# Memory-augmented attention beside a SiLU layer: weight pieces issued earlier, x tiles loaded from another queue, a new order of the work

## The chip, the cores and the metric

The kernel runs on one core of one Trainium2 chip. The core has a matrix engine (PE, with its weight loads shown apart as PEld), a vector engine (DVE), an activation engine (ACT), a general engine (POOL) and a sync engine (SP); each works through its own instructions in order, and semaphores join them. DMA transfers are issued from the queue of one of the engines, here SP and, for two tiles, ACT. The metric is the device time of one execution in microseconds, as the median of several runs; less is better.

## The reference

The input x has 2048 rows of 512 values. It is normalised once, and the result goes to an attention with a running memory and to a dense layer with SiLU. Both outputs are added to x. All data is bf16.

```
xn = _layernorm(x, axis=-1)
return x + _A_ref(xn, A_wq, A_wk, A_wv, A_wo, A_beta) + _B_ref(xn, B_w1, B_w2)
...
for s in range(N):                                  # N = 4 segments of 512 rows, 32 heads of 16
    logits = einsum('bhqd,bhkd->bhqk', qs, ks) * scale + mask
    a_dot = einsum('bhqk,bhkd->bhqd', softmax(logits), vs)
    a_mem = einsum(phi(qs), M) / (einsum(phi(qs), z) + 1e-06)
    o = g * a_mem + (1.0 - g) * a_dot
    M = M + einsum(phi(ks), vs);  z = z + sum(phi(ks))
...
out = einsum('bsf,fd->bsd', silu(einsum('bsd,df->bsf', xn, w1)), w2)      # 512 -> 1792 -> 512
```

Here phi(t) is t + 1 for positive t and exp(t) otherwise, and g is the sigmoid of beta, per head.

## The kernel before

The rows are taken in 16 tiles of 128, four tiles to a segment. The order of all work is written out by hand in the string ORDER (line 16): each word names a piece, the numbers behind it say of which segment, tile or part, and the loop at line 895 calls the pieces in that order. Every engine gets its instructions in this order and works them off one by one; an engine can run ahead of the others as far as its semaphores let it. So a word that only issues a DMA from SP runs when SP comes to it, which may be long before PE comes to the word that follows.

The words, as far as the prediction needs them:

- `xs`, or `xc` and `xd`: mean and variance of a tile of x on DVE (lines 283 to 292). `xq` and `xi` make the reciprocal root of the first four tiles on ACT and DVE (301, 304), `xg` that of four tiles at once on POOL (294). `Nv` normalises a tile on DVE (312). `X` and `Xa` or `Xv` turn the first four tiles on PE and copy them (831, 838); `XD` turns each of the others by a DMA transpose on SP (847).
- `k`, `q`, `v`, `h`: the products with wk, wq, wv and w1 on PE, in two or four parts; `ka`/`kv`, `qa`/`qv`, `va`/`vv` copy them out on ACT or DVE; `ha` (tanh, line 482) and `hv` make SiLU on ACT and DVE. `K` masks k by head on POOL (377).
- `S`: one of 72 batches of scores (line 699). Its products go into `psS`, of which there is one (line 701, four of the eight banks of the accumulator memory); ACT then takes the exponential of all 128 x 2048 values (721), and POOL clears what the causal mask forbids (735). `E` and `O` multiply 16 times each by v (line 760), `Ev`/`Ea` and `Ov`/`Oa` copy the result.
- `fa`, `ga`: exponentials of k and q for phi on ACT; `t`, `m`, `mv`, `mw`: the memory; `s`, `r`, `R`, `w`, `W`, `z`, `d`, `n`: sums, reciprocals and weights, with DMAs on SP that spread them.
- `o`, `oc`, `od`: products with w2 (index 0 to 13) and wo (14 to 17) for an output tile, with all 512, with 256 and with 128 columns (line 618); `oh` is a half of the last tile. `xl` loads a tile of x again to be added (601), `st` adds and stores a tile (606), `sh` half of the last one (653).
- `lw0.k` and `lw1.k` issue the loads of piece k of w2 and of wo on SP (883). `busy` gives PE products on zeros until the first real work (852). `kind`, `odd`, `omask`, `bmask` make small constants on DVE, `tb` has the table of the exponential loaded (307).

The products of the other words use four narrow products of 32 columns of weights beside each other, or one whole one, as the loop at line 895 finds it; listed by shape, a product of 512 columns has a mean of 380 ns either way. Scores are tiled by rows, so each S changes the tiling and changes it back.

At the start, SP issues tiles 0 and 2 of x, ACT tiles 1 and 3, each ahead of the weights wv, wk, wq, w1 and the other tiles of x on SP (lines 163 to 184). The first activation on ACT comes later, in line 211, a root of a constant that POOL makes; it brings the table load with it.

Of the kernel before, what the change touches and what calls it, by code (L numbers as in the profile page):

```python
# [25 lines left out]
S12 v1.1.3 fa0.3 Ov0 q1.0.0 q1.0.1 vv1.1 hv0.6 E1 k1.2.0 k1.2.1 k1.2.2 Ev1
S7 lw0.1 h0.7.0 fv0.0 q1.1.0 q1.1.1 q1.0.2 k1.2.3 kv1.2 h0.7.1 q1.1.2 q1.1.3 q1.0.3 qv1.1 fa0.2
S9 h0.5.0 h0.5.1 h0.5.2 h0.5.3 h0.8.0 h0.8.1 Nv8 Nv11 XD11 qv1.0 fv0.3 lw0.13 Nv10 XD8 XD10 ha0.5 hv0.5 t0.3 h0.7.2 lw1.3 fp0.2 h0.8.2 h0.8.3 ha0.8 Om0 hv0.8
S10 gp1.1 q1.2.0 q1.2.1 q1.2.2 h0.7.3 Nv9 ha0.7 q1.2.3 k1.0.0 qv1.2 lw0.5 lw1.2 k1.0.1 k1.0.2 XD9 k1.0.3 h0.10.0 kv1.0
S13 h0.10.1 O1 hv0.7 Ov1 q1.3.0 q1.3.1 q1.3.2 k1.3.0 q1.3.3 qv1.3 ga1.1  # L30
S11 fv0.2 h0.10.2 fp1.0 k1.3.1 t0.2 t0.0 k1.3.2 k1.3.3 xs15 kv1.3 h1.1.0 h1.1.1 h0.10.3 k1.1.0 lw0.0 ha0.10 h1.1.2 h1.1.3 ha1.1 hv0.10
S15 k1.1.1 hv1.1 h0.9.0 h0.9.1 h0.9.2 E2 K1.0 h0.9.3 ha0.9 h1.2.0 xs14 gv1.1 hv0.9 h1.2.1
S14 h1.2.2 h1.2.3 Ev2 k1.1.2 k1.1.3 kv1.1 xs12 ha1.2 hv1.2 O2 k2.2.0 lw0.4
S17 h1.10.0 h1.10.1 k2.2.1 kv2.2 lw1.0 h1.10.2 h1.10.3 ha1.10 gate h0.11.0 h0.11.1 h0.11.2 Ov2
S16 h0.12.0 h0.11.3 ha0.11 h0.12.1 h0.12.2 hv1.10 E3 Om2 Ev3 lw0.2 lw0.7 xl0.0 K1.1 hv0.11 k2.1.0 h0.12.3 ha0.12 K1.2
S20 k2.1.1 h0.13.0 h0.13.1 h0.13.2 kv2.1 hv0.12 O3 fp1.2 Ov3 m0.2 mv0.2 h0.13.3 fa1.0 Om1
S18 q2.1.0 q2.1.1 v2.2.0 m0.0 qv2.1 v2.2.1 lw0.3 ha0.13 fv1.0 K1.3
S19 mv0.0 k2.0.0 k2.0.1 hv0.13 v2.1.0 v2.1.1 kv2.0 fa1.2 h1.11.0
S22 vv2.2 sv0 r0.1 q2.3.0 lw0.8 vv2.1 h1.11.1 h1.11.2 xs13 xg12.4 o0.2.12 h1.11.3 q2.3.1 ha1.11 hv1.11 o0.2.7
S24 qv2.3 o0.2.4 lw0.11 od0.2.11.2 h1.8.0 h1.8.1 h1.8.2 h1.8.3 o0.2.13 h1.0.0 lw0.6 oc0.2.6.0 o0.2.1 od0.2.11.1 ha1.8 r0.2 r0.0  # L40
S25 E4 o0.2.2 h1.0.1 r0.3 w0 o0.2.8 z0.1 h1.0.2 h1.0.3 xl0.2 ha1.0 z0.2 hv1.8 Ev4 od0.2.11.0 h1.7.0 Nv15
S21 hv1.0 K2.1 h1.4.0 h1.7.1 h1.4.1 fv1.2 h1.7.2 h1.7.3 ha1.7 Nv12 XD12 hv1.7 q2.0.0 q2.0.1 XD15
S23 o0.2.3 qv2.0 h1.4.2 h1.4.3 ha1.4 o0.2.0 od0.2.11.3 fp1.1 z0.0 zv0.1 O4 z0.3 Ov4 k2.3.0
S26 zv0.2 fp1.3 k2.3.1 h1.9.0 h1.9.1 h1.9.2 h1.9.3 hv1.4 ha1.9 o0.0.8 K2.0 kv2.3 hv1.9 o0.0.5 o0.0.15
S31 E5 o0.0.4 bmask o0.0.2 od0.0.1.1 oc0.0.3.0 oc0.0.7.1 h1.13.0 Ev5 o0.0.10 fa1.3 h1.13.1
S28 Om3 O5 o0.0.6 Ov5 o0.0.13 Nv13 od0.0.1.0 o0.0.9 h1.13.2 h1.13.3 ha1.13 hv1.13 h1.3.0
S27 oc0.0.7.0 fv1.3 h1.3.1 oc0.0.3.1 h1.3.2 h1.3.3 xl0.3 od0.0.1.2 oc0.2.6.1 zv0.0 h1.12.0 ha1.3 h1.12.1 h1.12.2 hv1.3 XD13 gp1.2 t1.3 h1.12.3 ha1.12 hv1.12 Om5 oc0.2.10.1
S29 zv0.3 od0.0.1.3 o0.0.12 oc0.2.10.0 o0.0.16 o0.0.0 o0.2.15 o0.2.16 E6 fa1.1 o0.3.9 o0.3.15
S30 o0.3.16 o0.2.5 Ev6 o0.3.17 o0.3.6 o0.2.9 fv1.1 o0.1.14 o0.2.14 gp2.3 o0.2.17 st0.2 od0.1.8.3 t1.1 ga1.2 od0.1.8.1 gv1.2 oc0.3.1.1 gp1.0
S33 oc0.1.9.1 o0.0.17 o0.3.0 o0.3.12 Nv14 od0.1.8.0 o0.0.11 o0.1.17 XD14 o0.1.15 o0.0.14 t1.2 st0.0 ga1.0 gv1.0 t1.0 o0.3.14 od0.3.2.1  # L50
S32 O6 Ov6 o0.1.7 v2.0.0 o0.1.11 v2.0.1 vv2.0 oc0.3.3.1 ga2.3 fp2.1 gv2.3
S35 q2.2.0 q2.2.1 o0.1.3 qv2.2 o0.1.16 E7 Ev7 fa2.1 oc0.1.9.0
S34 mw0.0 fv2.1 o0.3.7 h1.6.0 o0.3.10 h1.6.1 o0.3.8 od0.3.2.2 od0.3.2.0 Om4 h1.6.2 h1.6.3 oc0.1.2.1 o0.3.11 ha1.6 hv1.6 gp1.3
S40 mw0.2 ga1.3 K2.3 o0.1.1 o0.3.4 O7 Ov7 gv1.3 q3.1.0 q3.1.1 xl0.1 qv3.1 oc0.3.3.0
S42 k3.1.0 o0.1.10 o0.3.13 k3.1.1 kv3.1 oc0.3.1.0 od0.3.2.3 oc0.1.2.0 o0.3.5 m1.2 mv1.2
S36 o0.1.13 o0.1.4 ga2.2 st0.3 od0.1.8.2 s1 sv1 gp2.2 v2.3.0 o0.1.5 K2.2 xl1.1 o1.2.12 r1.0 o0.1.0 m1.0
S37 fp2.0 v2.3.1 o0.1.12 Om6 mv1.0 vv2.3 o0.1.6 o1.2.10 Om7 q3.3.0 fa2.0 q3.3.1
S38 r1.1 qv3.3 h2.8.0 h2.8.1 v3.3.0 t2.1 ha2.8 v3.3.1 r1.3 r1.2 w1 o1.2.8 z1.3
S39 st0.1 hv2.8 od1.2.0.0 od1.2.0.2 vv3.3 z1.1 q3.2.0 q3.2.1 E8 Ev8 v3.0.0 d1.3
S41 qv3.2 v3.0.1 h2.11.0 o1.2.1 d1.2 h2.11.1 k3.0.0 ha2.11 zv1.3  # L60
S49 vv3.0 h1.5.0 h1.5.1 fv2.0 t2.0 h1.5.2 h1.5.3 ha1.5 hv2.11 o1.2.3 gv2.2 k3.0.1 kv3.0 z1.2 E9 hv1.5
S44 fp2.2 k3.2.0 ga2.1 k3.2.1 o1.2.13 xl1.2 v3.2.0 v3.2.1 Ev9 kv3.2 dv1.3
S43 vv3.2 zv1.1 h2.7.0 n1.3 nv1.3 gp2.1 h2.7.1 ha2.7 zv1.2 q3.0.0 q3.0.1
S48 qv3.0 d1.1 d1.0 O8 Ov8 o1.2.6 dv1.2 h2.5.0 h2.5.1 ha2.5 hv2.7 o1.2.4 oc1.2.11.1
S45 oc1.2.2.1 z1.0 K3.2 O9 hv2.5 h2.1.0 Ov9 dv1.0 h2.1.1 dv1.1 ha2.1 h2.12.0
# [868 lines left out]
```

## Time and profile before

| | us |
|---|---|
| median of 3 runs (221.83 to 222.88) | 221.88 |
| the profiled execution | 220.66 |
| its span | 218.9 |
| busy in it: POOL | 126.9 |
| busy in it: DVE | 180.0 |

The median is that of unprofiled executions; rows of the profile belong to the profiled execution, whose span runs from its first to its last instruction. All times of rows count from the start of that span. Busy shares say which engine is loaded over the whole; where the time goes is read from the chain of waits and from the timeline, which lists instructions in order of start, with several of a kind merged ("x8"). In a row "out<-in" are the tiles written and read, and in brackets stands the idle time ahead of it and what ended it.

### The profile page before, as it was taken

What the parts mean: (1) busy time and instruction counts of PE and PEld (TensorE: products, weight loads), DVE (VectorE), ACT (ScalarE), POOL (GpSimd) and SP (SyncE); (2) the same over time, 40 slices, a digit from 0 to 9 for tenths busy, and PEclk for the clock granted to TensorE, in tenths of its full rate; (3) what the DMA queues carried; (4) which work ended last, traced back from release to release, by engine and by line L of the source; (5) the groups of instructions that cost most, each with busy time, mean ns of one, the idle gap of its engine ahead of it and who ended that gap; (6) DMA issues with size and microseconds to landing.
All of it is one profiled execution on the core that took longest, in us unless ns stands there. A gap on an engine that the chain in (4) does not pass through costs nothing.

```text
span 218.9 us, 9451 instructions
## 1 busy us (share of the span) xinstructions
PE 213.7 (98%) x4081; PEld 116.7 (53%) x4081; DVE 180.0 (82%) x367; ACT 184.0 (84%) x174; POOL 126.9 (58%) x189
## 2 busy tenths in 40 slices
...
DMA packets 33530, 19.62 MB, mean 90 GB/s; under 512 B 14928, under 2 KB 33488, under 8 KB 33488
## 3 DMA queue, kind: packets, MB, share of 16 engines
...
q10 hardware_dynamic: 288, 0.26, 0.4%
q14 instruction: 10, 0.08, 0.1%
...
## 4 chain that ended last, share of the span: by engine, by line
PE 88%; ACT 8%; issue 2%; DVE 0%
PE ps L335 21%; PE psO L337 17%; PE ps L337 16%; PE psS L715 10%; PE psO L335 9%; PE psV L782 8%; ACT Pb L721 4%; PE psS L337 4%; PE psS L855 2%; ACT th L482 1%; ACT ex L413 1%; PE psM L442 1%; ACT L308 1%; ACT xnT L842 0%; ACT Vz L396 0%
## 5 line engine op out<-in xcount | busy, mean ns | idle before, releaser
L721 ACT ACTIVATE Pb<-psS 128x2048 bf16<-128x2048 f32 x72 | 135.2, 1878 | 4.0 <-PE psS L715 2.7
L735 POOL TENSOR_SCALAR_AFFINE_SELECT Pb<-Pb 128x512 bf16<-128x512 bf16 (+1 forms) x72 | 60.5, 841 | 29.6 <-ACT Pb L721 26.8
L487 DVE SCALAR_TENSOR_TENSOR hT<-th,ps 128x512 bf16<-128x512 bf16 x56 | 37.6, 678 | 12.7 <-ACT th L482 12.0
L337 PE MATMUL psO<-w_sb,hT 128*32 128x512 bf16 (+2 forms) x712 | 43.5, 324 | 0.0
L735 POOL TENSOR_SCALAR_AFFINE_SELECT lows<-Pb 64x512 bf16<-64x512 bf16 (+1 forms) x40 | 23.6, 589 | 26.2 <-ACT Pb L721 21.2
L335 PE MATMUL ps<-xnT,w_sb 128*128 128x512 bf16 (+1 forms) x157 | 34.8, 335 | 0.0
L482 ACT ACTIVATE th<-ps 128x512 bf16<-128x512 f32 x56 | 32.6, 596 | 2.3 <-PE ps L337 1.6
L337 PEld LDWEIGHTS <-hT 128*32 128x32 bf16 x880 | 22.2, 97 | 14.5 <-issue 2.3
L337 PE MATMUL ps<-xnT,w_sb 128*32 128x512 bf16 (+1 forms) x492 | 27.8, 340 | 0.0
L715 PE MATMUL psS<-qT,k 32*128 32x64 bf16 (+3 forms) x512 | 23.0, 233 | 0.3 <-ACT qT L389 0.2
L715 PEld LDWEIGHTS <-k 32*128 32x128 bf16 x512 | 9.7, 92 | 22.7 <-issue 22.2
L335 PE MATMUL psO<-w_sb,hT 128*128 128x512 bf16 (+2 forms) x88 | 21.7, 323 | 0.0
L782 PE MATMUL psV<-Pb,Vz 128*32 128x448 bf16 (+7 forms) x512 | 21.3, 287 | 0.0
L782 PEld LDWEIGHTS <-Vz 128*32 128x32 bf16 x768 | 15.7, 97 | 9.3 <-issue 1.3
L335 PEld LDWEIGHTS <-w_sb 128*128 128x128 bf16 x157 | 14.2, 98 | 11.9 <-issue 2.6
L381 POOL TENSOR_SCALAR k<-kT,pm_odd 128x512 bf16<-128x512 bf16 x16 | 11.7, 734 | 8.0 <-ACT kT L375 7.0
L337 PEld LDWEIGHTS <-w_sb 128*32 128x32 bf16 x492 | 12.4, 97 | 7.0 <-issue 0.8
L715 PE MATMUL psS<-qT,kT 16*128 16x448 bf16 (+3 forms) x256 | 14.7, 269 | 0.0
L611 DVE SCALAR_TENSOR_TENSOR o_out<-psO,x_res 128x512 bf16<-128x512 f32 x14 | 9.6, 688 | 5.9 <-PE psO L337 2.7
L335 PE MATMUL ps<-wv_sb,xnT 128*128 128x512 bf16 x49 | 12.9, 380 | 0.5 <-ACT xnT L842 0.5
L335 PEld LDWEIGHTS <-hT 128*128 128x128 bf16 x88 | 8.2, 98 | 8.8 <-issue 1.3
L819 DVE CAST odd<-psV 128x512 bf16<-128x512 f32 x15 | 10.3, 685 | 2.9 <-PE psV L782 2.8
...
## 6 DMA issues: line engine op xcount, KB each, us to landing
...
```

Of the source, the lines that this page charges most:

```text
L335: return [nc.tensor.matmul(out, lhsT=lhsT, rhs=rhs, start=start, stop=stop, skip_group_check=True)]
L337: nc.tensor.matmul(out[c : c + 32], lhsT=lhsT[:, c : c + 32], rhs=rhs, start=start, stop=stop, tile_position=(0, c), skip_group_check=True,)
L381: nc.gpsimd.tensor_scalar(out=to, in0=frm, scalar1=keep[:, 0:1], scalar2=1.0, op0=ALU.mult, op1=ALU.mult)
L482: nc.scalar.activation(out=th[:], in_=sts[s]["h", ft][:, :], func=AF.Tanh, scale=0.5)
L487: nc.vector.scalar_tensor_tensor(out=st["hT"][:, ft, :], in0=st.pop(("th", ft))[:], scalar=1.0, in1=st.pop(("h", ft))[:, :], op0=ALU.add, ...
L611: out = nc.vector.scalar_tensor_tensor(out=o_out[:], in0=st.pop(("psO", j)), scalar=0.5, in1=st["x", j][:], op0=ALU.mult, op1=ALU.add)
L715: nc.tensor.matmul(psS[:, g, c : c + q2 - q1], lhsT=keys[rows], rhs=st["qT"][rows, dt, q1:q2], start=True, stop=True, tile_position=(32 * ...
L721: exp = nc.scalar.activation(out=blocks(Pb, b).rearrange("p x g c -> p g x c"), in_=psS[:, :, :].rearrange("p g (x c) -> p g x c", c=block ...
L735: over[id(Pb)].append(nc.gpsimd.affine_select(out=out, in_=in_, compare_op=ALU.is_ge, fill=0.0, base=base, pattern=pattern, channel_multip ...
L782: nc.tensor.matmul(psV[32 * g : 32 * g + 32, q0 : q0 + nq], lhsT=Vzs[s % 2][:, kt, 4 * dt + g, par : par + 2, :].rearrange("p a d -> p (a ...
L819: copy(out=odd[:], in_=sts[s].pop(("psV", 1))[:, :])
L855: nc.tensor.matmul(idle[:, 0:P], lhsT=zraw[:, 0:P], rhs=zraw[:, 0:P], start=True, stop=True)
```

## The change

Three things are edited.

1. **Loads at the start.** SP issues tile 0, then wv in two halves, then tile 3, then the rest as before. ACT first takes a root of a zero (a new activation behind the clearing of `zraw`; the one of line 211 stays), which brings the table load to the front of its instructions, and then issues tiles 1 and 2.

```diff
     load_x(nc.sync, 0, 1)
-    load_x(nc.scalar, 1, 1)
-    load_x(nc.sync, 2, 1)
-    load_x(nc.scalar, 3, 1)
...
     load_w(nc.sync, wv_sb, A_wv, 0, 2)
     load_w(nc.sync, wv_sb, A_wv, 2, 4)
+    load_x(nc.sync, 3, 1)
     load_w(nc.sync, wk_sb, A_wk, 0, 4)
...
     nc.vector.memset(zraw[:], 0.0)
     spare = cpool.tile([P, 1], F32, name="spare")
+    nc.scalar.activation(out=spare[:], in_=zraw[:, 0:1], func=AF.Sqrt)
+    load_x(nc.scalar, 1, 1)
+    load_x(nc.scalar, 2, 1)
```

2. **The head of the order.** `kind`, `odd` and `omask` go from the front to a place behind the first products; 41 dummies instead of 44; tile 1's `xd` stands ahead of tile 0's `Nv`, as its `xc` did already; `ka0.1` stands ahead of the first S and `qa0.1` behind it (the first line of ORDER, wrapped here):

```diff
-kind odd omask ones0 ones1 zeros xc0 xd0 xc1 xq0 xi0 Nv0 xd1 busy44 xc2 xq1 X0.1 Xa0.1 v0.0.0 xi1 Nv1 X1.1 v0.0.1 xd2 xq2 Xa1.1 v0.0.2 xs3 xi2 v0.0.3
-v0.1.0 v0.1.1 Nv2 xq3 xi3 v0.1.2 va0.0 Nv3 tb X2.1 Xv2.1 k0.1.0 X3.1 Xv3.1 v0.1.3 va0.1 k0.0.0 xs5 xs4 k0.0.1 k0.0.2 k0.0.3 q0.0.0 q0.0.1 q0.0.2
-q0.0.3 ka0.0 K0.0 fa0.0 qa0.0 q0.1.0 q0.1.1 q0.1.2 xs6 q0.1.3 qa0.1
+ones0 ones1 zeros xc0 xd0 xq0 busy41 xc1 xi0 xd1 xq1 Nv0 X0.1 Xa0.1 v0.0.0 xc2 xi1 Nv1 X1.1 xd2 xq2 v0.0.1 v0.0.2 v0.0.3 xs3 Xa1.1 xi2 Nv2 v0.1.0 xq3
+xi3 Nv3 v0.1.1 v0.1.2 va0.0 X2.1 Xv2.1 v0.1.3 X3.1 Xv3.1 tb k0.1.0 k0.0.0 k0.0.1 k0.0.2 bmask k0.0.3 k0.1.1 odd kind va0.1 ka0.0 q0.0.0 K0.0 q0.0.1
+q0.0.2 q0.0.3 k0.1.2 xs7 k0.1.3 xs4 fa0.0 q0.1.0 fp0.0 xs5 qa0.0 ka0.1
```

3. **The rest of the order.** It is new from end to end, with the same words. The first batches now come as S2 S0 S3 S1, the last as S69 S71 S70. The words `lw` stand further ahead of the first use of their piece: before, `lw0.11` and `lw0.6` stood in the same period as that use (behind S24) and `lw0.8` two periods ahead; now the least is four periods, for `lw0.9`, and seven for the next ones. The first lines behind the head, with `K0.1`, `XD4` and the first `lw`:

```diff
-S3 k0.3.0 k0.3.1 k0.3.2 k0.3.3 kv0.3 xs7 xg4.4 Nv7 k0.1.1 k0.1.2 k0.1.3 ka0.1 Nv4 K0.3 XD7 h0.0.0 h0.0.1
-S0 q0.2.0 v0.2.0 v0.3.0 v0.3.1 q0.2.1 K0.1 h0.0.2 h0.0.3 ha0.0 q0.2.2 XD4 q0.2.3 hv0.0 Nv5 fp0.0
-S1 v0.3.2 v0.2.1 v0.2.2 qv0.2 v0.3.3 h0.1.0 h0.1.1 vv0.3 h0.1.2 h0.1.3 ha0.1 v0.2.3 vv0.2
-S2 lw1.1 k0.2.0 k0.2.1 lw0.12 tanh k0.2.2 k0.2.3 hv0.1 q0.3.0 kv0.2 h0.2.0 h0.2.1 q0.3.1 xs11 Nv6 fa0.1 h0.3.0
-S4 h0.2.2 h0.2.3 v1.3.0 XD5 ha0.2 xs10 v1.3.1 v1.3.2 v1.3.3 vv1.3 h0.3.1 q0.3.2 lw0.9 h0.3.2
...
+S2 v0.2.0 q0.1.1 v0.2.1 omask v0.2.2 v0.2.3 xs6 k0.2.0 k0.2.1 fa0.1 k0.2.2 vv0.2 fv0.0 xg4.4 k0.3.0 Nv6 XD6 Nv5
+S0 q0.1.2 q0.1.3 qa0.1 k0.3.1 k0.3.2 k0.2.3 kv0.2 q0.2.0 k0.3.3 kv0.3 q0.2.1 q0.2.2 Nv7 K0.2
+S3 q0.2.3 qv0.2 XD5 h0.2.0 h0.2.1 h0.2.2 h0.2.3 Nv4 ha0.2 h0.0.0 h0.0.1 K0.1 h0.3.0 xs10
+S1 v0.3.0 h0.3.1 h0.3.2 lw1.1 hv0.2 v0.3.1 v0.3.2 v0.3.3 vv0.3 h0.3.3 ha0.3 hv0.3 h0.0.2 h0.0.3 fp0.1 ha0.0
+S4 fp0.3 xs9 h0.1.0 q0.3.0 h0.1.1 h0.1.2 hv0.0 h0.1.3 ha0.1 xs11 q0.3.1 v1.1.0 v1.1.1 XD7 q0.3.2 q0.3.3
+S6 v1.2.0 hv0.1 fa0.3 v1.2.1 v1.2.2 v1.2.3 lw0.2 v1.1.2 v1.1.3 E0 qv0.3
+S5 vv1.2 vv1.1 v1.3.0 fv0.3 h0.4.0 v1.3.1 v1.3.2 v1.3.3 XD4 fa0.2 lw0.0 Ev0 v1.0.0 xs8 xg8.4 v1.0.1 t0.0 v1.0.2 v1.0.3
...
```

The start of the last line of ORDER, which holds all that follows the last S, and its end, before and now (wrapped):

```diff
-S71 hv3.10 R0.0 E15 Ev15 o2.1.14 o2.3.16 o2.1.15 h3.13.0 h3.13.1 ha3.13 o2.1.17
...
-n3.2 Om15 zv3.3 o3.1.15 o3.1.4 o3.2.7 o3.2.13 nv3.3 xl3.1 oh15.0 o3.1.8 oh2.0 o3.1.17 oh14.1 o3.2.5 o3.1.13 o3.1.0 zv3.2 nv3.2 o3.0.16 oh16.1 o3.2.0
-od3.1.1.3 o3.1.14 o3.1.16 st3.1 oh17.1 o3.2.16 o3.0.6 od3.0.2.2 o3.2.17 st3.2 oh17.0 o3.0.17 o3.0.8 o3.0.11 st3.0 oh0.0 oh1.1 oh11.1 oh12.1 oh11.0
-oh15.1 oh9.1 oh6.1 oh8.1 sh1 oh10.0 oh7.0 oh16.0 oh6.0 oh13.0 sh0
...
+S70 o2.3.14 o2.1.14 o2.1.4 o2.3.8 hv3.10 od2.1.9.0 R0.3 E15 Ev15 od2.3.10.1 R0.0 h3.3.0 h3.3.1 ha3.3 o2.1.15 hv3.3 o3.2.0 oh0.0
...
+n3.0 xl3.1 o3.0.5 oh8.0 o3.1.15 od3.1.1.3 o3.0.4 xl3.2 zv3.0 o3.0.9 o3.2.16 oh0.1 nv3.0 o3.2.14 o3.0.14 oh17.1 o3.2.3 o3.1.14 o3.1.3 o3.1.9 o3.1.0
+o3.1.8 o3.2.15 st3.2 oh14.1 o3.0.15 oh15.1 sh1 o3.1.16 st3.1 o3.0.8 od3.0.2.1 oh15.0 o3.0.6 o3.0.11 st3.0 oh16.0 oh2.0 oh11.0 oh17.0 oh4.0 oh10.0
+oh14.0 sh0
```

Counted in products of 512 columns (a part of k, q, h or v of segment 0 or 1 is one, of the later segments two; S, X, n, s and `o` are one, E and O two and a half, m, `oc` and `oh` a half, `od` a quarter), the two orders hold:

| | before | changed |
|---|---|---|
| ahead of the first S | 25 | 25 |
| from the first to the last S | 734 | 736.75 |
| from the last S on | 119 | 116.25 |
| periods (S to next S) with no, one, two words of ACT behind S | 3, 56, 12 | 1, 58, 12 |

134 lines of the change are left out of this document (66 added, 68 removed).

## The prediction

> **What bounds the kernel now.** I read the page first, for the engines' busy time and the chain that ended last.
>
> ```profile
> span 218.9 us, 9451 instructions
> PE 213.7 (98%) x4081; PEld 116.7 (53%) x4081; DVE 180.0 (82%) x367; ACT 184.0 (84%) x174; POOL 126.9 (58%) x189
> PE 88%; ACT 8%; issue 2%; DVE 0%
> L721 ACT ACTIVATE Pb<-psS 128x2048 bf16<-128x2048 f32 x72 | 135.2, 1878 | 4.0 <-PE psS L715 2.7
> ```
>
> PE is never free and carries the chain; ACT with its 72 exponentials is the second load. How the two share the time is seen in one period of the timeline (start, duration, engine, line).
>
> ```profile
> 76.11 1.88 ACT L721 ACTIVATE Pb<-psS 128x2048 bf16<-128x2048 f32 x1
> 77.88 0.59 ACT L482 ACTIVATE th<-ps 128x512 bf16<-128x512 f32 x1
> 78.04 0.21 PE L715 MATMUL psS<-qT,k 32*128 32x64 bf16 x4
> 78.50 1.88 ACT L721 ACTIVATE Pb<-psS 128x2048 bf16<-128x2048 f32 x1
> ```
>
> There is one `psS`: the scores of the next batch start (78.04) when the exponential has read it (76.11 + 1.88 = 77.99), and the next exponential follows at 78.50. The period is 2.39 us, and in its 0.51 us of scores one other ACT operation (`th`) is hidden; a second makes the period longer. PE fills the same period with products. So I count the time in three stretches: to the first exponential, the 71 periods, and what follows the last exponential.
>
> ```profile
> 12.79 1.88 ACT L721 ACTIVATE Pb<-psS 128x2048 bf16<-128x2048 f32 x1
> 144.90 1.88 ACT L721 ACTIVATE Pb<-psS 128x2048 bf16<-128x2048 f32 x1
> 190.07 1.87 ACT L721 ACTIVATE Pb<-psS 128x2048 bf16<-128x2048 f32 x1
> 213.43 0.61 PE L337 MATMUL psO<-w_sb,hT 128*32 128x512 bf16 x8
> 213.86 0.73 PE L337 MATMUL psS<-w_sb,hT 128*32 128x256 bf16 x20
> 214.04 1.55 PE psS L337 x56
> 215.59 0.02 issue
> ```
>
> The 71 periods take 177.28 us (2.50 each), the tail 25.52 us from 190.07 to PE's end at 215.59, the drain 3.3 us from there to 218.9. Two products of 512 columns (x8, four narrow ones each) go by in 213.86 - 213.43 = 0.43 us: 0.215 us is PE's unit. Counting the words of ORDER in it, the order before holds 25 units ahead of the first S, 734 between first and last, 119 behind the last S: 119 x 0.215 = 25.6, so the tail is PE at its peak. The middle is 734 x 0.215 = 157.8 and 19.5 us over that, 0.274 per S (the scores' change of tiling and the waits for `psS`).
>
> **The new order in the middle and the tail.** The new order has the same 878 units, 72 S and 144 changes of tiling. It holds 25 units ahead, 736.75 in the middle, 116.25 behind. The tail so loses 2.75 x 0.215 = 0.6 us. What the middle gains has two bounds. If PE sets it, with the same 0.274 per S, it is 0.6 longer. If the cycle of ACT sets it, nothing changes: 12 periods have two ACT words in both orders, the rest one or none (59). Before, the 54 periods up to 144.90 average 2.45, near the cycle's 2.39, and the last 17 average 2.66, where PE is overfull; the new order overfills its last periods too. I take +0.4, nearer to PE's bound, for these rows are where the units went, and keep 0 to +0.6. Below 0 it can go too: a few periods of the old middle are longer than their cycle and their units ask for (0.1 to 0.2 us each in four places, 0.6 in all), and a new order has its irregularities elsewhere or nowhere: -0.5 is the low end.
>
> **The pieces of w2 and wo.** Before, the word `lw0.6` stands directly ahead of its use; that is not when it runs.
>
> ```profile
> 60.37 2.87 SPq L168 DMA_DIRECT2D w_sb<-in_B_w_dram  x4
> 68.05 0.54 PE L335 MATMUL psO<-w_sb,hT 128*128 128x256 bf16 x3
> PE psS L855 <- DVE zraw L187: 1.1, 1, 1.1
> PE ps L335 <- ACT xnT L842: 0.5, 1, 0.5
> PE psS L715 <- ACT qT L389: 0.2, 1, 0.2
> ```
>
> SP had run ahead: the last four pieces were issued from 60.37 to 63.24, the first use of the last (68.05) came 4.8 us later, and the list of PE's waits (the last three rows, all of it) has no weight. So issuing them earlier removes nothing here: 0. What it adds is SP time at other places, 2.87/4 = 0.7 us an issue, behind S1 to S18, where the transposes of xn queued behind them have two or more periods in hand: 0 as well, and half a microsecond if one of them is late once.
>
> **The head.** The rows of the first microseconds:
>
> ```profile
> 0.78 0.90 ACTq L158 DMA_DIRECT2D x_lo<-in_A_x_dram  x2
> 0.79 0.87 SPq L158 DMA_DIRECT2D x_lo<-in_A_x_dram  x2
> 1.10 4.61 PEld L855 LDWEIGHTS <-zraw 128*128 128x128 bf16 x44 [1.10 <-DVE zraw L187]
> 1.40 1.23 DVE L261 MEMSET lows<- 64x1408 uint32 x1 [0.35 <-issue]
> 1.71 1.28 ACT L211 ACT_TABLE_LOAD   x1 [1.71 <-PEq L918]
> 3.01 0.20 ACT L211 ACTIVATE spare<-eps 128x1 f32<-128x1 f32 x1
> 3.48 0.15 DVE L234 CAST omask<-pm_odd 128x1 int32<-128x1 f32 x1
> 3.55 0.69 DVE L285 BATCH_NORM_STATS2 stats<-x_lo 128x6 f32<-128x512 bf16 x1
> 4.37 0.66 DVE L285 BATCH_NORM_STATS2 stats<-x_lo 128x6 f32<-128x512 bf16 x1
> 5.13 0.41 DVE L314 TENSOR_SCALAR xn_t<-x_lo,mv_all,rstd_all 128x512 bf16<-128x512 bf16 x1
> 5.46 0.18 DVE L288 BATCH_NORM_AGGREGATE mv_all<-stats 128x2 f32<-128x6 f32 x1
> 5.67 0.41 PEld L836 LDWEIGHTS <-xn_t 128*128 128x128 bf16 x4
> 1.50:2.00 0.50, 0.50 (x7) 0.50 (x6) 0.50 (x1) 0.29 (x1) 0.43 (x5) 1.00 0.44 45
> 2.50:3.00 0.50, 0.50 (x7) 0.50 (x6) 0.43 (x4) 0.50 (x1) 0.50 (x2) 1.00 1.03 359
> 4.50:5.00 0.50, 0.50 (x7) 0.50 (x6) 0.50 (x2) 0.29 (x1) 0.00 (x0) 1.00 0.80 197
> 8.10 0.58 ACT L396 CAST Vz<-ps 128x512 bf16<-128x512 f32 x1
> 11.47 0.69 DVE L285 BATCH_NORM_STATS2 stats<-x_hi 128x6 f32<-128x512 bf16 x1 [1.70 <-DMA x_hi<-in_A_x_dram]
> ```
>
> (The three rows with a colon are windows: the last two figures are the DMA share and GB/s.) Tile 0's statistics start at 3.55 right behind `omask`; with `kind`, `odd` and `omask` moved back they can start up to 0.9 earlier, when DVE has cleared `lows` (2.63). `kind` and `odd` land in DVE's 1.7 us of idle time ahead of 11.47, and `omask` has one operation of 0.15: 0. But PE is in order: the first transposes (5.67) stand behind the dummies, which end at 5.71, and three dummies fewer give 3 x 4.61/44 = 0.31. That is the most that the head can gain.
>
> It gains it only if x's tile 1 is there. Its DMA now stands behind the table load and one activation on ACT: 0.8 + 1.28 + 0.2 = 2.3 instead of 0.78. From an issue to the first bytes it took about 1 us (0.78 to the window from 1.5). Then 128 KB at half of 197 to 359 GB/s, beside `wv` on SP's queue, take 0.7 to 1.3: landing at 4.0 to 4.6. A bound from above: tile 0, issued at 0.79, was used at 3.55, 2.76 later, which gives 5.1; from below, if the DMA doesn't wait for the activation, it starts at about 1 and nothing is late. On DVE tile 1's statistics stand ahead of tile 0's reciprocal and normalisation, as before, and now its mean (`xd1`) does too, so a late tile 1 holds all. From its start to the transposes were 1.3 us (4.37 to 5.67), now 1.45 with the 0.18 us of `xd1` in between: a landing at 3.9 gives the full -0.31, at 4.2 it is even, at 4.4 it costs 0.2. Tile 2 lands some 0.7 later, before DVE wants it. From 8.10 ACT works without a gap to 12.79, so what the transposes lose, the first exponential loses. I take +0.1, with -0.31 to +0.9 as ends.
>
> The Trainium skill ("ScalarE: Activation LUTs", What ACT_TABLE_LOAD costs) puts a drain of about 1.38 us behind every switch of table. The trace doesn't show it here: the load ends at 2.99 and the activation starts at 3.01. By the page tile 1 would be issued at 3.7, and the time be up to 1.4 higher than the forecast, 223.7. As no row shows such a gap, I give that rule 0.02, which lies within the chance of the late tile below.
>
> **The end.**
>
> ```profile
> 213.33 0.69 DVE L611 SCALAR_TENSOR_TENSOR o_out<-psS,x_res 128x512 bf16<-128x512 f32 x1
> 214.09 0.69 DVE L611 SCALAR_TENSOR_TENSOR o_out<-psO,x_res 128x512 bf16<-128x512 f32 x1
> 215.62 0.42 DVE o_half L658
> ```
>
> Before, the last half store's DVE operation starts 0.03 after PE's end. In the new order `st3.2 sh1 st3.1 st3.0 sh0` stand close together: from the last product of `st3.2` PE has 2 units to `sh1`, 1 to `st3.1`, 3.75 to `st3.0`, 3.5 to `sh0`: 10.25 x 0.215 = 2.2 us. DVE needs three operations 0.76 apart (213.33 to 214.09) and one of about 0.48: 2.76. `sh0` waits 0.56; by durations alone (3 x 0.69 + 0.42 = 2.49) 0.29. I take +0.5, with 0.3 to 0.7 as ends (a 128 KB store instead of a 64 KB one is also in flight just ahead).
>
> **Sum.** Head +0.1, middle +0.4, tail -0.6, end +0.5: +0.4 on the profiled execution, which took 220.66 (span 218.9 and 1.76 around it) and so 221.06. The median of the runs is 221.88, 1.22 higher; with the same difference 222.3.
>
> **Rivals.**
> - **Tile 1 late (slower).** One mechanism: the wait of DVE for the tile behind the table load. It decides from a landing at 4.2 on and costs one for one. For it: 2.3 + 2.76 = 5.1 is +0.9. Against: 2.76 is a bound, since DVE was busy until 3.55. With the other terms (+0.4 - 0.6 + 0.5) it is +1.2: 223.1.
> - **Faster.** The tile lands by 3.9 (-0.31), the middle stays at its cycle or loses its odd periods (0 to -0.5), the tail is 0.6 shorter, the end costs 0 to 0.3: -0.6 to -1.4, 220.9. For it: the units are only moved, and 0.31 of dummies do go. Against: the overfull periods late in the new middle (up to 13.5 units, 2.9 us).
> - **No effect.** The weights were never late, the units are the same, all terms cancel: 221.9.
> - **A late edge.** `K0.1` now stands one period ahead of S4 instead of four; a K or a bank late once makes one period 0.5 to 1.0 longer: with the sum 223.0.
>
> **Chances.** Forecast 0.41, tile 1 late 0.20, late edge 0.10, faster 0.21, no effect 0.08. The range reaches from the low end of the faster case, but for its last tenth or two (220.6), to the dear end of the late tile with some late edge (223.7). Half a per cent is 1.1 us, about what a measurement of this kernel can tell from no change: below 220.77 falls two thirds of the faster case, 0.14; above 222.99 the better part of the late tile, half of the late edge and the upper end of the forecast, 0.25; between them 0.61.
>
> **What would show it.** Transposes at 5.4 to 5.9; first exponential at 12.6 to 13.0; 71 periods of 177.3 to 177.9; 24.9 us from the last exponential to PE's end; `sh0`'s operation 0.3 to 0.6 behind PE's end. It is wrong if tile 1 lands beyond 5, or if PE shows a new wait in the middle.

## The result and the profile after

| | before | changed |
|---|---|---|
| median of 18 and of 15 runs (lowest to highest), us | 221.66 (220.80 to 222.88) | 223.44 (221.75 to 224.75) |
| ratio, with its 95% interval | 1 | 1.0073 [1.0048, 1.0098] |
| the profiled execution, us | 220.66 | 222.36 |
| its span, us | 218.9 | 220.7 |
| first exponential starts | 12.79 | 12.63 |
| the 71 periods to the last exponential | 177.28 | 179.22 |
| last exponential to PE's end | 25.50 | 25.04 |
| PE's end to the end of the span | 3.4 | 3.8 |

The change makes the kernel slower by 0.7%, which is 1.6 us (0.0073 x 221.66), and its runs lie further apart: 3.0 us from lowest to highest against 2.1. Slow runs (three more of the changed kernel, 225.32 to 226.83, two of them at a granted clock of 0.989 and 0.991, and one of e2 below) stand in none of the figures. The two profiled executions differ by 1.7 us (220.66 to 222.36). The stretches are those of the prediction, read in the same way from the timeline; three of the four changed by half a microsecond or less, and the middle by +1.94. The profiled execution of before lies 1.0 us below the median, so small differences between single profiles say little.

The page of the changed kernel, its busy times, shares of the chain and the exponentials (out<-in, count | busy, mean ns | idle before):

```profile
PE 213.4 (97%) x3952; PEld 115.5 (52%) x3952; DVE 179.7 (81%) x367; ACT 184.6 (84%) x175; POOL 126.0 (57%) x189
PE 89%; DVE 4%; ACT 3%; POOL 1%; issue 1%; DVEq 0%
L722 ACT ACTIVATE Pb<-psS 128x2048 bf16<-128x2048 f32 x72 | 135.2, 1878 | 4.7 <-PE psS L716 3.3
```

The work is the same: PE 213.4 us against 213.7, ACT's exponentials 135.2 in both. What is new stands in the second line: DVE now carries 4% of the chain that ended last, where it had 0%, and POOL 1%. So somewhere PE waited for them. The list of PE's waits says where (engine, tile and line waiting <- what ended it: us in total, times, longest):

```profile
PE ps L336 <- DVE kT L376: 1.3, 1, 1.3
PE psS L856 <- DVE zraw L185: 1.1, 1, 1.1
PE ps L336 <- ACT xnT L843: 0.5, 1, 0.5
PE psM L443 <- DVE o_out L612: 0.3, 1, 0.3
PE psS L716 <- ACT qT L390: 0.2, 1, 0.2
```

The first and the fourth row weren't there before. The windows view puts the first one in its place (window, its length, busy us of PE, PEld, DVE, ACT, POOL with instructions, granted clock, DMA share, GB/s):

```profile
12.63:21.05 8.42, 7.16 (x81) 4.86 (x80) 7.16 (x17) 7.23 (x7) 5.59 (x10) 1.00 0.80 244
191.85:216.90 25.05, 25.05 (x636) 15.66 (x628) 15.74 (x33) 3.06 (x3) 0.66 (x1) 1.00 0.22 62
```

In the first three periods PE stands still for 8.42 - 7.16 = 1.26 us; in the tail it has no gap at all, as before. The chain of waits through that place (start, us, what):

```profile
14.58 0.66 POOL Pb L736
...
15.33 0.51 POOL rstd_all L297
...
15.91 1.03 POOL rstd_all L300
...
16.97 1.34 DVE xn_t L315 x2
18.31 0.61 DVE kT L376
...
18.96 1.69 PE ps L336 x14
```

Read from below: PE's products of `h0.2` (18.96) need a bank of the accumulator memory, and the bank is free when DVE has copied `k0.2` out of it (`kv0.2`, 18.31). That copy is short and could have run at 16.3 (it does in e1, below), but in the new order it stands on DVE behind `Nv6` and `Nv5`. `Nv6` needs the reciprocal roots of tiles 4 to 7 (`xg4.4`, lines 297 and 300), which POOL makes, and POOL has them queued behind the mask of the first batch (14.58), which can't start ahead of the end of the first exponential (12.63 + 1.88 = 14.51). So a short copy that PE needs soon hangs on ACT's first exponential by way of POOL and two normalisations that nobody is waiting for yet. The exponential isn't all of it: the statistics that the roots are made from are complete at 14.46 only (14.28 + 0.18 on DVE, below), and behind the mask the roots start at 15.33, 0.87 later. The timeline of the changed kernel shows the same place on DVE and PE, and the exponential that comes late by it:

```profile
14.28 0.18 DVE L289 BATCH_NORM_AGGREGATE mv_all<-stats 128x2 f32<-128x6 f32 x1
16.97 1.34 DVE L315 TENSOR_SCALAR xn_t<-x_hi,mv_all,rstd_all 128x512 bf16<-128x512 bf16 x2 [1.19 <-POOL rstd_all L300]
18.96 1.69 PE L336 MATMUL ps<-xnT,w_sb 128*128 128x256 bf16 x14 [1.26 <-DVE kT L376]
21.05 1.88 ACT L722 ACTIVATE Pb<-psS 128x2048 bf16<-128x2048 f32 x1 [0.41 <-PE psS L716]
```

The third exponential starts at 17.43, so this period has 21.05 - 17.43 = 3.62 us where its neighbours have 2.4 (S3 in the table below).

Before, DVE waited for the same roots even longer. The timeline of the kernel before:

```profile
13.89 0.66 DVE L375 CAST kT<-ps 128x512 bf16<-128x512 f32 x1
16.83 1.03 DVE L314 TENSOR_SCALAR xn_t<-x_hi,mv_all,rstd_all 128x512 bf16<-128x512 bf16 x2 [1.47 <-POOL rstd_all L299]
```

There the copy `kv0.3` stood ahead of `Nv7` and ran at 13.89, and PE's list of waits has no row for what stood behind: 1.47 us of waiting that cost PE nothing.

### The profile page after: what moved, and what is told of

Read it like the earlier page. It is cut to its first block, busy times and chain, and to the rows that moved or that the text cites. A ratio compares the mean times of both kernels' runs of the same rounds, so it can differ in the third digit from the quotient of the medians.

```text
span 220.7 us, 9188 instructions
## 1 busy us (share of the span) xinstructions
PE 213.4 (97%) x3952; PEld 115.5 (52%) x3952; DVE 179.7 (81%) x367; ACT 184.6 (84%) x175; POOL 126.0 (57%) x189
## 4 chain that ended last, share of the span: by engine, by line
PE 89%; DVE 4%; ACT 3%; POOL 1%; issue 1%; DVEq 0%
PE ps L336 26%; PE psO L338 16%; PE ps L338 13%; PE psS L716 10%; PE psO L336 9%; PE psV L783 8%; PE psS L338 3%; PE psS L856 2%; DVE o_out L612 1%; ACT Pb L722 1%; PE psM L443 1%; DVE phiQT L590 1%; DVE xn_t L315 1%; ACT L309 1%; DVE hT L488 1%
## 5 line engine op out<-in xcount | busy, mean ns | idle before, releaser
L722 ACT ACTIVATE Pb<-psS 128x2048 bf16<-128x2048 f32 x72 | 135.2, 1878 | 4.7 <-PE psS L716 3.3
L338 PE MATMUL psO<-w_sb,hT 128*32 128x512 bf16 (+2 forms) x684 | 39.3, 320 | 0.0
L336 PE MATMUL ps<-xnT,w_sb 128*128 128x512 bf16 (+1 forms) x168 | 37.1, 337 | 1.3 <-DVE kT L376 1.3
L338 PEld LDWEIGHTS <-hT 128*32 128x32 bf16 x852 | 20.5, 97 | 12.6 <-issue 1.9
L338 PE MATMUL ps<-xnT,w_sb 128*32 128x512 bf16 (+1 forms) x448 | 25.4, 338 | 0.0
L336 PE MATMUL psO<-w_sb,hT 128*128 128x512 bf16 (+2 forms) x95 | 24.8, 330 | 0.0
L336 PEld LDWEIGHTS <-w_sb 128*128 128x128 bf16 x168 | 15.6, 98 | 13.7 <-issue 3.0
L336 PE MATMUL ps<-wv_sb,xnT 128*128 128x512 bf16 x56 | 15.3, 380 | 0.5 <-ACT xnT L843 0.5
L336 PE MATMUL ps<-xnT,wq_sb 128*128 128x512 bf16 (+1 forms) x67 | 15.0, 329 | 0.0
L338 PE MATMUL psO<-wo_sb,oT 128*32 128x512 bf16 x160 | 14.5, 380 | 0.0
L336 PE MATMUL ps<-xnT,wk_sb 128*128 128x512 bf16 (+1 forms) x67 | 14.2, 329 | 0.0
```

The costliest lines, as they stand in the source:

```text
L336: return [nc.tensor.matmul(out, lhsT=lhsT, rhs=rhs, start=start, stop=stop, skip_group_check=True)]
L338: nc.tensor.matmul(out[c : c + 32], lhsT=lhsT[:, c : c + 32], rhs=rhs, start=start, stop=stop, tile_position=(0, c), skip_group_check=True,)
L722: exp = nc.scalar.activation(out=blocks(Pb, b).rearrange("p x g c -> p g x c"), in_=psS[:, :, :].rearrange("p g (x c) -> p g x c", c=block ...
```

## The experiments

The theory from the two traces: **the wait of `Nv6` with `kv0.2` behind it** costs 1.2 us, the second new wait (line 443) some more, and the rest is within the prediction's terms. The rivals: the loads at the start (another time at which x lands), the earlier pieces of weights, the crowded end. e1 to e4 ran on one chip, e5 to e8 on a second and e9 to e12 on a third, each set beside runs of the kernel before on the same chip. All stretches are read from the profiled executions, in us (S1, S3, S36 and S37 are single periods; the middle is all 71; the drain goes from PE's end to the end of the span, with spans taken to the hundredth, 218.95 before and 220.66 changed):

| kernel | ratio to before, 95% | first exponential | middle | S3 | S1 | S36 | S37 | drain | span |
|---|---|---|---|---|---|---|---|---|---|
| before | | 12.79 | 177.28 | 2.41 | 2.53 | 2.47 | 2.38 | 3.38 | 218.9 |
| changed | 1.0073 [1.0048, 1.0098] | 12.63 | 179.22 | 3.62 | 2.72 | 3.01 | 2.37 | 3.76 | 220.7 |
| e11, changed again | 1.0057 [1.0028, 1.0085] | 12.65 | 180.80 | 3.72 | 2.73 | 3.00 | 2.38 | 3.92 | 222.4 |
| e1 | 1.0016 [0.9997, 1.0034] | 12.48 | 178.51 | 2.39 | 3.09 | 3.00 | 2.38 | 4.08 | 220.1 |
| e2 | 1.0048 [1.0025, 1.0071] | 12.55 | 178.44 | 2.90 | 2.73 | 2.54 | 2.77 | 3.66 | 219.7 |
| e10 = e1 + e2 | 1.0012 [0.9991, 1.0033] | 12.59 | 177.99 | 2.38 | 2.76 | 2.54 | 2.77 | 4.17 | 219.8 |

### e1: the normalisations behind the copies

The edit, in the changed kernel: the three words go behind `kv0.2` and `kv0.3`.

```diff
-S2 ... fv0.0 xg4.4 k0.3.0 Nv6 XD6 Nv5
-S0 ... k0.2.3 kv0.2 q0.2.0 k0.3.3 kv0.3 q0.2.1 q0.2.2 Nv7 K0.2
+S2 ... fv0.0 xg4.4 k0.3.0
+S0 ... k0.2.3 kv0.2 q0.2.0 k0.3.3 kv0.3 Nv6 XD6 Nv5 q0.2.1 q0.2.2 Nv7 K0.2
```

> The changed kernel with one edit: Nv6 XD6 Nv5 stand behind kv0.2 and kv0.3 instead of ahead of them. Theory (DVE waits 1.19 us for POOL's root in front of the two k copies, and PE waits 1.3 us for the bank that the first copy frees): the third period falls from 3.62 to 2.4-2.6, the time by 1.0 to 1.3 us against the changed kernel, so a ratio to the kernel before of about 1.002 (changed kernel: 1.0073). Rival (the period is long because segment 1's tiles come late or the loads at the start collide): the third period stays above 3.3 and the ratio at 1.007. Second rival (the wait only moves to the transposes XD6, XD5 that now come some 0.7 us later): a period between the fifth and the ninth grows by 0.5 or more.

Measured: 1.0016 [0.9997, 1.0034]. The timeline of e1:

```profile
16.25 1.28 DVE L376 CAST kT<-ps 128x512 bf16<-128x512 f32 x2
17.39 1.69 PE L336 MATMUL ps<-xnT,w_sb 128*128 128x256 bf16 x14
17.45 1.98 DVE L315 TENSOR_SCALAR xn_t<-x_hi,mv_all,rstd_all 128x512 bf16<-128x512 bf16 x3
20.07 0.38 PE L336 MATMUL ps<-wv_sb,xnT 128*128 128x512 bf16 x1 [0.45 <-DVE qT L390]
```

The copies run at 16.25 without waiting, the products of `h0.2` follow at 17.39 with no gap, and S3 falls from 3.62 to 2.39. A part comes back one period later: three normalisations in a row take 1.98 us and hold the copy of q behind them, so PE waits 0.45 (S1 3.09 instead of 2.72; in e10, with the same words there, S1 has 2.76). Three moved words and one period: in this set of runs most of the loss goes. The ratio falls to 1.0016, with an interval that doesn't touch that of the first measurement of the changed kernel (1.0073) and overlaps that of the second (1.0057); how much of the loss the wait makes over all runs is taken up behind e11.

### e2: the store ahead of the weights

The second new wait is that of `m1.0` (line 443) for the bank that the store `st0.1` has to read first. The timeline of the changed kernel:

```profile
111.50 0.73 DVE L541 TENSOR_SCALAR rz<-ri,gate 128x256 bf16<-128x256 f32 x1
112.16 0.68 DVE L612 SCALAR_TENSOR_TENSOR o_out<-psO,x_res 128x512 bf16<-128x512 f32 x1
112.89 0.38 PE L443 MATMUL psM<-Vz,phiK 128*32 128x32 bf16 x32 [0.34 <-DVE o_out L612]
```

`w1` (`rz`) stands on DVE ahead of the store. The edit puts the store first:

```diff
-S36 k3.0.0 xl3.0 r1.2 w1 z1.2 ha2.8 o0.1.11 o0.1.10 st0.1 E9
+S36 k3.0.0 xl3.0 r1.2 ha2.8 o0.1.11 o0.1.10 st0.1 w1 z1.2 E9
```

> The changed kernel with one edit: st0.1 stands ahead of w1 and z1.2 on DVE. Theory (m1.0 waits for the bank that st0.1 frees, with r1.2 and w1 ahead of it on DVE): the period from S36 falls from 3.01 to 2.4, the time by 0.4 to 0.6 us, ratio about 1.005. Rival (m1.0 waits for something else, or the later w1 holds up the products that need z1.2): the period stays at 3.0, or another one within 15 us behind it grows by as much; ratio 1.007.

Measured: 1.0048 [1.0025, 1.0071]; the wait of line 443 is gone from the list, and S36 falls from 3.01 to 2.54. But S37 behind it rises from 2.37 to 2.77: together 5.38 before the edit and 5.31 after it. Of 0.47 us that one period gained, the next gave back 0.40. A wait as long as the old one stands in the trace of e2 at the next copy on DVE:

```profile
112.69 1.02 PE L336 MATMUL ps<-wv_sb,xnT 128*128 128x512 bf16 x3 [0.34 <-DVE oraw L813]
```

That copy (`Ev9`) stands behind the store and `w1` in either order, so DVE reaches it no sooner. The rival of the expectation (the next period grows by as much) is nearly what happened; the ratio came out as expected, but not by this edit, whose two periods gain 0.07. The rest of the difference of this trace from the changed kernel's lies in S3, which the edit doesn't touch:

```profile
16.64 0.89 DVE L315 TENSOR_SCALAR xn_t<-x_hi,mv_all,rstd_all 128x512 bf16<-128x512 bf16 x2 [0.25 <-POOL rstd_all L300]
18.17 1.69 PE L336 MATMUL ps<-xnT,w_sb 128*128 128x256 bf16 x14 [0.55 <-DVE kT L376]
```

POOL had the roots at 16.60 instead of 16.93, the two normalisations took 0.89 instead of 1.34, and PE waited 0.55 instead of 1.26. The first wait differs from execution to execution: it is 0.55 in e3 as well.

### e3: the end spread; e4: all three

In e3 the last stores stand further apart:

```diff
-... o3.2.14 o3.0.14 oh17.1 o3.2.3 o3.1.14 o3.1.3 o3.1.9 o3.1.0 o3.1.8 o3.2.15 st3.2 oh14.1 o3.0.15 oh15.1 sh1 o3.1.16 st3.1 o3.0.8 od3.0.2.1 oh15.0
-o3.0.6 o3.0.11 st3.0 oh16.0 oh2.0 ...
+... o3.2.14 o3.0.14 o3.1.14 o3.1.3 o3.1.9 o3.1.0 o3.1.8 o3.1.16 st3.1 o3.2.3 o3.2.15 st3.2 o3.0.15 o3.0.8 od3.0.2.1 o3.0.6 o3.0.11 st3.0
+oh17.1 oh14.1 oh15.1 sh1 oh15.0 oh16.0 oh2.0 ...
```

> The changed kernel with the last words in another order: st3.1, st3.2 and st3.0 stand further apart and further ahead of sh0. Theory (the drain of 3.8 us instead of 3.3 comes from stores that queue on SP and DVE ahead of the last half): the drain from PE's end to the span's end falls to 3.2-3.4, the time by 0.3 to 0.6 us, ratio about 1.005. Rival (the drain's length is that of the last DMA alone): drain 3.7 or more, ratio 1.007.

Measured: 1.0087 [1.0054, 1.0119], from 8 runs; the drain is 3.59, between the 3.2 to 3.4 of the theory and the 3.7 of its rival. The edit brings nothing that can be measured. In e4 the edits of e1, e2 and e3 stand together.

> The changed kernel with all three edits. If the three stalls are what made it slower and they add up, the time falls by 1.7 to 2.4 us, to a ratio of 0.996 to 1.000: first exponential at 12.6, middle 177.2 to 177.6, tail 25.0, drain 3.3. If other waits take their place, the ratio stays above 1.003.

Measured: 1.0032 [1.0009, 1.0055], middle 178.09, drain 4.04. The expected 0.996 to 1.000 was missed: the three edits don't bring back the time of before. With the same end as e3 the drain is 0.45 longer, so one profile of an end says little; this is taken up below.

### e5 and e6: the loads alone, the pieces alone

e5 is the kernel before with part 1 of the change only (ACT's early root, tiles 1 and 2 behind it, tile 3 behind `wv`).

```diff
-    load_x(nc.scalar, 1, 1)
-    load_x(nc.sync, 2, 1)
-    load_x(nc.scalar, 3, 1)
...
+    load_x(nc.sync, 3, 1)
...
+    nc.scalar.activation(out=spare[:], in_=zraw[:, 0:1], func=AF.Sqrt)
+    load_x(nc.scalar, 1, 1)
+    load_x(nc.scalar, 2, 1)
```

> The kernel before with the new loads alone (early root on ACT, tiles 1 and 2 behind it on ACT, tile 3 behind wv on SP); its order is the old one. Theory (the loads do no harm: ACT's two issues start at 1.09, while the table is still loading, and the head of the order gains only by what stands ahead of tile 0): first exponential within 0.2 us of 12.79, ratio 0.998 to 1.002. Rival (late tiles): first exponential 13.0 or later, ratio 1.002 or more.

Measured: 1.0004 [0.9982, 1.0026]; first exponential 12.94, middle 177.28, drain 3.75. No effect of the loads alone can be seen.

e6 is the kernel before with eleven of the words `lw` moved ahead to the periods that they have in the new order, for instance:

```diff
-S24 qv2.3 o0.2.4 lw0.11 od0.2.11.2 h1.8.0 h1.8.1 h1.8.2 h1.8.3 o0.2.13 h1.0.0 lw0.6 oc0.2.6.0 ...
+S24 qv2.3 o0.2.4 od0.2.11.2 h1.8.0 h1.8.1 h1.8.2 h1.8.3 o0.2.13 h1.0.0 oc0.2.6.0 ...
-S17 h1.10.0 h1.10.1 k2.2.1 kv2.2 lw1.0 h1.10.2 h1.10.3 ha1.10 gate h0.11.0 h0.11.1 h0.11.2 Ov2
+S17 h1.10.0 h1.10.1 k2.2.1 kv2.2 lw1.0 h1.10.2 h1.10.3 ha1.10 gate h0.11.0 h0.11.1 h0.11.2 Ov2 lw0.7 lw0.8 lw0.11
```

> The kernel before with eleven lw words moved ahead, each to the period in which the changed kernel has it; nothing else. Theory (no product ever waited for w2 or wo): ratio 0.998 to 1.002, the middle within 0.4 us of 177.3. Rival (SP's issues in between delay transposes or spreads): ratio 1.003 or more. Rival (weights were late in many runs): ratio below 0.998.

Measured: 0.9996 [0.9978, 1.0014]; middle 177.94, drain 3.81. The earlier pieces alone do nothing to the time either. The middle of this one profile misses the expected 0.4: it is 0.66 above before, in three periods (S1 0.25, S18 and S46 0.18 each), and PE's waits have no weight among them.

### e7 and e12: the old loads under the new order

e7 is e1 with part 1 of the change undone (the diff of e5 the other way round).

> The changed kernel with Nv6 XD6 Nv5 behind the k copies, and with the old loads (tiles 1 and 3 first on ACT, tile 2 on SP, no early root); order new otherwise. Theory (the new order starts tile 0 earlier whichever way the tiles are loaded): first exponential at 12.4 to 12.8, ratio within 0.002 of that with the new loads (1.0016). Rival (the head's gain is that of the loads): first exponential at 12.8 to 13.0 and the time 0.2 to 0.4 us longer.

Measured: 1.0059 [1.0032, 1.0086], which is 0.4% above e1 and not within the expected 0.002; the first exponential starts at 12.68, as expected. Taken alone, this would say that the new loads gain 0.4% under the new order. But e1 ran on another chip, so e12 repeats the comparison beside e10 on one chip: e10 with the same part undone.

> The same as with two edits, with the old loads (tiles 1 and 3 first on ACT, tile 2 on SP, no early root), to set beside it on one chip. Theory (the new loads bring tile 0 some 0.4 us earlier and the head 0.2): ratio 0.0005 to 0.0015 above that of the new loads. Rival (the loads are worth 0.4%, as the earlier pair of runs on two chips had it): 0.003 or more above. Second rival (no difference at all).

Measured: 1.0023 [0.9999, 1.0048] against 1.0012 [0.9991, 1.0033] for e10. No difference between the loads can be seen there. The trace of e7 shows what else it had: its first wait is gone (the copies are again ahead), but another wait stands at 119 us, of the kind seen in e11 below. Whether that accounts for the 0.4% isn't shown.

### e8: the same fault put into the kernel before

If a copy behind a waiting normalisation is the cause, it must cost in the old order too. `kv0.3` goes behind `Nv7`, and nothing else moves:

```diff
-S3 k0.3.0 k0.3.1 k0.3.2 k0.3.3 kv0.3 xs7 xg4.4 Nv7 k0.1.1 ...
+S3 k0.3.0 k0.3.1 k0.3.2 k0.3.3 xs7 xg4.4 Nv7 kv0.3 k0.1.1 ...
```

> The kernel before with one word moved: kv0.3 stands behind Nv7 instead of ahead of xs7. Theory (a copy that frees a bank, queued on DVE behind a normalisation that waits for POOL's root, stops PE): one of the first three periods grows from 2.4 by 0.8 to 1.5 us, ratio 1.004 to 1.007. Rival (such a wait is caught up within the next periods, and the changed kernel's is of another kind): ratio below 1.002.

Measured: 1.0137 [1.0101, 1.0173], 3.0 us (0.0137 x 221.05, the median of the kernel before beside it), about twice what was expected. The timeline of e8:

```profile
16.71 0.41 DVE L314 TENSOR_SCALAR xn_t<-x_hi,mv_all,rstd_all 128x512 bf16<-128x512 bf16 x1 [1.82 <-POOL rstd_all L299]
17.04 0.68 DVE L375 CAST kT<-ps 128x512 bf16<-128x512 f32 x1
17.78 0.59 PE L335 MATMUL ps<-wv_sb,xnT 128*128 128x512 bf16 x2 [2.21 <-DVE kT L375]
```

The direction is that of the theory, the size was taken from the changed kernel's 1.26 us. Here PE needs the bank sooner: it stood at 15.57 already and waited 2.21 us, and the period S0 has 4.78 us. Not all of the 3.0 us need be the wait: three of the six runs have a granted clock of 0.989 to 0.992 (224.74 to 225.74), and the three at 0.999 (223.03 to 224.07) have a median 2.45 us above before. Either way, one word moved past three others makes a kernel slower by more than all of the change did.

### e9, e10 and e11: what is left, and the changed kernel again

e10 has the edits of e1 and e2 together. e9 has a third one, for the next irregular period (S49, 2.86 us):

```diff
-S49 hv2.1 h2.6.0 h2.6.1 ha2.6 gv2.1 o1.0.11 o1.2.10 o1.0.2 o1.2.16 o1.0.1 n1.1 nv1.1
-S47 hv2.6 o1.0.12 oc1.2.2.0 o1.0.16 n1.0 zv1.0 nv1.0 K3.0 o1.0.3 Om9 o1.2.5 o1.2.15 t2.2 E10 Ea10
+S49 hv2.1 h2.6.0 h2.6.1 ha2.6 gv2.1 o1.0.11 o1.2.10 o1.0.2 o1.2.16 o1.0.1
+S47 hv2.6 o1.0.12 oc1.2.2.0 n1.1 nv1.1 o1.0.16 n1.0 zv1.0 nv1.0 K3.0 o1.0.3 Om9 o1.2.5 t2.2 E10 Ea10 o1.2.15
```

> The changed kernel without its waits in the middle: Nv6 XD6 Nv5 behind the k copies, st0.1 ahead of w1, and n1.1 nv1.1 one period later (o1.2.15 behind E10). Theory (each wait is a bank whose copy is queued late on DVE; taking all away leaves an order as long as the one before): middle 177.4 to 178.0, no period above 2.95 but S68, ratio 0.997 to 1.000. Rival (what is left is not waits but the overfull periods late in the middle): middle 178.2 or more, ratio 1.001 or more.

> The changed kernel with the first two of these edits only. Theory: the two effects add (1.0016 with the first alone, -0.0025 from the second): ratio 0.998 to 1.001, middle about 178.0. Rival (the second edit does nothing once the first is made): 1.0016 or more.

> The changed kernel itself, beside the others on one chip. Theory (the wait of the third period hangs on when tiles 4 to 7 land and how long POOL's root takes, so it differs from execution to execution): third period between 2.9 and 3.7, ratio 1.005 to 1.009, and a wider spread of the times than in the kernels without that wait. Rival (a fixed wait): 3.6 again, and a spread like the others'.

Measured: e9 1.0024 [1.0000, 1.0049], e10 1.0012 [0.9991, 1.0033], e11 (the changed kernel without an edit, on the same chip) 1.0057 [1.0028, 1.0085]. e9 and e10 lie above the 0.997 to 1.000 and 0.998 to 1.001 that were expected; e11 lies within its range, with 3.72 us in the third period. The third edit moves the long period (S47 2.90 in place of S49 2.86; the middle is 178.04 against 177.99) and gains nothing. None of these is faster than the kernel before; e10 is as fast within its interval.

Over all runs, the four kernels that keep the first wait (changed, e11, e2, e3) have ratios of 1.0048 to 1.0087, 1.0066 in the mean, and the six without it (e1, e4, e7, e9, e10, e12) 1.0012 to 1.0059, 1.0028 in the mean. The difference is 0.8 us (0.0038 x 221.66), more than half of the loss. The traces agree: the four with the wait have 2.90, 2.91, 3.62 and 3.72 us in S3, 0.9 above e10's 2.38 in the mean. What is left, 0.6 us (0.0028 x 221.66), isn't traced to one place.

The trace of e11 shows the first wait once more and two waits that the first trace of the same kernel doesn't have:

```profile
PE ps L336 <- DVE kT L376: 1.4, 1, 1.4
PE ps L336 <- DVE Vz L397: 0.6, 1, 0.6
PE ps L336 <- DVE hT L488: 0.4, 1, 0.4
```

They lie at 122.79 and 124.56, and both copies stand on DVE behind one operation that waits for a DMA. From the timeline of e11, first DVE, then SP's queue, and the list of the issues of that tile (count: minimum, median, maximum in ns):

```profile
120.64 0.88 DVE L590 TENSOR_TENSOR phiQT<-spr,phiQT 128x512 bf16<-128x512 bf16 x1 [1.03 <-DMA spr<-rz]
115.56 5.92 SPq L568 DMA_DIRECT2D spr<-rz  x8
L568 SPq DMA_DIRECT2D spr<-rz x13: 602/637/1260, 112.4 to 125.6; - x13
```

and the same two places in the first trace of the changed kernel:

```profile
119.41 0.42 DVE L590 TENSOR_TENSOR phiQT<-spr,phiQT 128x512 bf16<-128x512 bf16 x1
115.42 5.26 SPq L568 DMA_DIRECT2D spr<-rz  x8
```

The new order has SP issue eight of these transfers in a row. Where each takes 0.60 to 0.65 us they are just in time (119.41, no wait); where one takes 1.26, the operation that needs them is late by 1.03, the copies behind it too, and S44 and S39 have 3.17 and 2.90 us instead of 2.44 and 2.43. It is the same fault as the first wait at another place, but it doesn't bite in every execution: the wait on DVE stands also in the traces of e4 (0.45), e7 (0.71) and e12 (0.49), each with one issue of 1.17 to 1.57 among the eight, and not in those of e1, e2, e3, e9 and e10. It costs a period only in e7 (S44 2.84) and e11; in e4 and e12 PE doesn't notice. Why an issue takes longer, and whether it holds the transfer up or is held up with it, stays open. Two profiles of one kernel differ by 1.2 us in these two periods; whether that is why the changed kernel's runs lie further apart isn't shown. The expected wider spread doesn't go with the first wait alone: e11 spreads over 2.4 us and e10 over 1.3, but e9 and e12, without that wait, over 2.1 and 2.7.

## Why the prediction was right in part, and where it failed

The forecast was +0.4 us, 222.3, with the range 220.6 to 223.7; the ratio puts the changed kernel at 1.0073 x 221.88 = 223.5 [222.9, 224.1] beside the median that was shown then. The direction was right, the likeliest size was not: 1.6 us instead of 0.4. That 223.5 lies inside the range is in part luck, for its dear end was drawn up mainly for a late tile 1, which was in time. By its own signs the prediction was wrong in the middle: it had named a new wait of PE there as the sign, and the trace has one; the 71 periods took 179.22 instead of 177.3 to 177.9.

- **The middle: the step that failed.** It took +0.4 (-0.5 to +0.6) from counts of units, of S and of ACT's words in each period; measured +1.94. With the first wait taken away (e10, which has the edit of e2 too) it is 177.99, +0.71, near the bound that it named for PE (2.75 x 0.215 = 0.6). The other 1.23 is nearly all S3 (3.62 against 2.38 in e10). The mechanism was there as the rival "a late edge": a bank that is late once makes one period 0.5 to 1.0 longer. It got a chance of 0.10 and was looked for at `K0.1`, which PE never waited for; in the trace it cost 1.2 us. What the step left out was to follow DVE's own order: the trace of before had the 1.47 us that DVE waited for POOL's roots, at 16.83, and the diff that the prediction had before it puts `Nv6` ahead of `kv0.2`. Both together name the place. Counting what each engine has to do in a period says nothing of the order in which DVE does it. Nor does the +0.71 bear out how the +0.4 was reasoned. The prediction took the late, overfull periods for the place that the units went to; of the 2.75 units 2.25 stand in the first 54 periods. These take 133.24 us in e10 against 132.11, and the last 17 take 44.75 against 45.17, shorter with half a unit more. That the sum lies near 0.6 may be chance.
- **The pieces of weights: 0.** Right for the time, as e6 shows (0.9996).
- **The head: +0.1 (-0.31 to +0.9).** Measured -0.16. The fear of a late tile 1 had its price from an issue at 2.3, behind the table load and an activation. The timeline of the changed kernel:

```profile
0.79 1.28 ACT L187 ACT_TABLE_LOAD   x1 [0.79 <-PEq L919]
1.09 0.88 ACTq L158 DMA_DIRECT2D x_lo<-in_A_x_dram  x2
2.08 0.20 ACT L187 ACTIVATE spare<-zraw 128x1 f32<-128x1 bf16 x1
3.04 0.69 DVE L286 BATCH_NORM_STATS2 stats<-x_lo 128x6 f32<-128x512 bf16 x1 [0.41 <-DMA x_lo<-in_A_x_dram]
3.87 0.66 DVE L286 BATCH_NORM_STATS2 stats<-x_lo 128x6 f32<-128x512 bf16 x1
5.35 0.47 PEld L837 LDWEIGHTS <-xn_t 128*128 128x128 bf16 x4
```

  ACT's queue issued both transfers from 1.09 on, while the table was still being loaded (0.79 to 2.07), so the bound "from below" of the prediction held: tile 1 was there at 3.87 without a wait, and the transposes started at 5.35 instead of 5.67. The drain of about 1.38 us that the Trainium skill ("ScalarE: Activation LUTs", What ACT_TABLE_LOAD costs) counts with every switch of table isn't behind the load in this trace either: the load ends at 2.07, the activation starts at 2.08. The gain itself is within what executions differ by: the first exponential starts at 12.48 to 13.20 in the eight profiles with the new head and the new loads (mean 12.74), and at 12.65 to 12.79 in the three with the old head and the old loads (before, e6 and e8, mean 12.70). At 13.20 (e9) it was tile 2 that came late, a case that the prediction had held to be safe; DVE waited for that tile in six of the eight, 0.2 to 1.06 us. The timeline of e9, and its list of PE's waits:

```profile
6.08 0.69 DVE L286 BATCH_NORM_STATS2 stats<-x_lo 128x6 f32<-128x512 bf16 x1 [1.06 <-DMA x_lo<-in_A_x_dram]
```

```profile
PE ptr L837 <- DVE xn_t L315: 0.6, 1, 0.6
```

  With the old loads under the new order (e12) it starts as late, at 13.20, by other waits (the first transposes and wk, 0.5 and 0.4), so neither way of loading is always in time.
- **The tail: -0.6.** Measured -0.46 in every profile with the new order (25.04 or 25.05 against 25.50). The units were the right measure here, where PE has no gap.
- **The end: +0.5 (0.3 to 0.7).** Measured +0.38 in these two profiles (3.76 against 3.38), but not for the reason given. The prediction had DVE late by three stores; the timeline of the changed kernel shows PE, DVE and SP:

```profile
216.37 1.61 SPq L617 DMA_DIRECT2D out_dram<-o_out  x2
216.61 0.28 PE L338 MATMUL psS<-wo_sb,oT 128*32 128x256 bf16 x4
216.95 0.43 DVE L659 SCALAR_TENSOR_TENSOR o_half<-psS,x_res 128x256 bf16<-128x256 f32 x1
218.07 0.40 SPq L663 DMA_DIRECT2D out_dram<-o_half  x1
```

  PE ends at 216.89 and `sh0`'s operation starts 0.06 later, not 0.3 to 0.6. It ends at 217.38, and its store is issued at 218.07 only, because SP was issuing two others until 217.98. Before, too, the last store stood behind a long issue, the two half stores taking 1.27 us, the first of them 0.80:

```profile
215.52 1.27 SPq L662 DMA_DIRECT2D out_dram<-o_half  x2
```

  That the size came out within the stated ends, by another queue, is luck. It differs between executions: the four profiles with the old end have drains of 3.38 to 3.81 (mean 3.60), the eight with the new one 3.66 to 4.40 (mean 4.04), and e3 and e4 with the spread end 3.59 and 4.04. The means differ by 0.44, the ranges overlap, and no ratio shows it: what the end costs is not settled beyond that.

So the sum without the first wait would have been -0.16 + 0.71 - 0.46 + 0.38 = +0.5, near the forecast; e10 measures +0.3 (0.0012 x 221.71), with an interval from -0.2 to +0.7, and all six kernels without that wait +0.6 in the mean.
